# Linear attention and a squared-ReLU layer on one core: every SBUF tile begins 32 bytes past a multiple of 128

## The chip, the core and the metric

The kernel runs on one core of a Trainium2 chip. Five engines take part, each with its own list of instructions: TensorE (PE; its weight loads are listed apart as PEld), VectorE (DVE), ScalarE (ACT), GpSimd (POOL) and SyncE (SP), which here issues all transfers. SBUF is the on-chip memory of 128 partitions; a tile takes the same byte range in each partition, and that range's beginning is what this case is about. The metric is the device time of one execution in microseconds, median of three runs.

## The reference

Two stages follow each other. The first is linear attention over 4 batches, 4 heads, 1088 positions and 32 channels, with features that are products of two 8-wide projections (64 features). The second is a layer from 128 to 2048 and back, with `s * relu(h)**2 + b` between.

```python
def phi(x):
    a = np.einsum('rd,bhsd->bhsr', S1, x)
    b = np.einsum('rd,bhsd->bhsr', S2, x)
    return np.einsum('bhsi,bhsj->bhsij', a, b).reshape(*x.shape[:-1], r * r)
q_p, k_p = (phi(q), phi(k))
kv = np.einsum('bhsf,bhsd->bhfd', k_p, v)
z = np.sum(k_p, axis=2)
num = np.einsum('bhsf,bhfd->bhsd', q_p, kv)
den = np.einsum('bhsf,bhf->bhs', q_p, z)[..., None] + 1e-06
x = num / den            # then (4352 tokens, 128)
r = np.maximum(x @ w_in, 0.0)
out = (s * (r * r) + b) @ w_out
```

All inputs and the output are float32.

## The kernel before

The 4352 tokens are cut into nine tiles, one of 256 and eight of 512 columns; tokens lie along the free dimension. For each batch b, `kvphase` (L240 on) makes the features of k, multiplies them with v (L268, 33 columns of weights: 32 channels and a column of ones) and turns the result into the tile `st`. For each token tile t, `direct_features` or `stored_features` makes the features of q (the latter through a store `qd<-abq` and loads `pq<-qd`, `br<-qd`), `attend` multiplies them with `st` and divides, and leaves `x`, split as `xh` + `xl` in the type fp32r (L405). `ffn` then does eight steps of two 128-wide pieces of the hidden layer. From the second tile on, each piece takes three matmuls of 512 columns into `hp` (weights wil, wih, wih; streamed operands xh, xh, xl) and three into `ops` (weights wol, woh, woh; streamed uh, uh, ul), all on line 446. Between them ReLU (L127 or L129), square (L133 or L135), a cast to `uh` (L111) and the rest `ul = u - uh` (L440) run on ScalarE or VectorE, by the table `ON_DVE`. The first tile uses plain float32 weights, the tiles `w24`. The weights come in as 64-bit numbers (`raw`), are put together into w24 (L117 to L187) and split into wih, wil, woh and wol (L111, L425).

The order of all work is written out by hand in the table `ORDER`: each word advances one generator by a step, and each engine's list follows from it. The step `z` is a keep-warm matmul of 512 columns that reads a constant again and again (L512).

SBUF tiles are laid out in the order in which the pools `const`, `p1`, `p2`, `p3` and `p4` ask for them, one behind the other. The program's addresses (bytes within a partition) are, before the change:

| tiles, in order | start past a multiple of 128 | why |
|---|---|---|
| s_raw (640 bytes), cst_sb (640), sk (320) | 0 | the pool begins at a multiple of 128 |
| sq, srep, kvt, wih, wil, woh, wol, bias, w24, s_bits (320) | 64 | behind the 320 bytes of sk |
| st, ph, dt, rc, rr, kt, vt, pq, br, kab, x, abq, u, xh, xl, ot, qt, uh, ul, raw | 0 | behind the 320 bytes of s_bits |

From rr on, the last row's tiles begin at a multiple of 256, too (kt and vt, pq and br, u, xh, xl, ot, qt, uh, ul and raw among them). The tile vt is asked for with 1216 floats where 1188 are used, and bias with 32 where one is used, so that what follows keeps its start. Operands begin inside their tiles at multiples of 128 bytes, but for the pieces of vt: a piece of 33 floats follows the next at 132 bytes, and a batch's second group of chunks begins 2640 bytes in (1584 in the first batch).

Of the kernel before, what the change touches and what calls it, by code (L numbers as in the profile page):

```python
# [9 lines left out]
F32 = mybir.dt.float32  # L10
F32R = mybir.dt.float32r
BF16 = mybir.dt.bfloat16
I32 = mybir.dt.int32
# [6 lines left out]
P = 128  # L20
# [44 lines left out]
NS = 32 * 2 + 2 * R  # L65
# [24 lines left out]
def attn_ffn_kernel(ctx: ExitStack, tc: tile.TileContext, qT, kT, vp, s80, cst, w_in, w_out, outT):  # L90
    nc = tc.nc
    PSUM = bass.MemoryType.PSUM
    const = ctx.enter_context(tc.tile_pool(name="const", bufs=1))
# [100 lines left out]
    def to_float(key, out, raw, bits):  # L194
        low, high = words(raw)
        scaled(key + "m", out, f32(high), 2.0 ** -112)
        yield
        scaled_up(key + "b", bits, low.bitcast(U32), 0.875 * 2.0 ** -29, 0.4999)
        yield
        join(out.bitcast(I32), out.bitcast(I32), bits)  # L200
        yield
        with_sign(out.bitcast(I32), high, out.bitcast(I32))
        yield

    s_raw = const.tile([P, 2 * NS], I32, name="s_raw")
    cst_sb = const.tile([P, NCST], F32, name="cst_sb")
    s_col = cst_sb[:, CS:CS + 1]
    b_col = cst_sb[:, CB:CB + 1]  # L210
    spread = cst_sb[:, CT:CT + P]
    sk = const.tile([P, NS], F32, name="sk")
    sq = const.tile([P, 64], F32, name="sq")
    srep = const.tile([P, 2, 64], F32, name="srep")

    def s_phase():
        bits = const.tile([P, NS], I32, name="s_bits")
        yield from to_float("s", sk, s_raw, bits)
        own = sk[:, 64:].rearrange("p (w r) -> p w r", w=2)
        nc.vector.tensor_copy(out=srep[:, 1].rearrange("p (i x) -> p i x", i=R),  # L220
                              in_=own[:, 1].unsqueeze(1).broadcast_to([P, R, R]))
        yield
        nc.vector.tensor_copy(out=srep[:, 0].rearrange("p (i x) -> p i x", i=R),
                              in_=own[:, 0].unsqueeze(2).broadcast_to([P, R, R]))
        yield
        nc.gpsimd.tensor_copy(out=sq.rearrange("p (w i h) -> p w h i", w=2, i=R),
                              in_=sk[:, :64].rearrange("p (w h i) -> p w h i", w=2, h=H))
        yield
# [286 lines left out]
    with tc.manual_schedule():  # L515
        gens = {"z": keep_warm(), "Ls": load_s(), "s": s_phase(), "Lcst": load_constants()}
        for b in range(B):
            gens[f"Lk{b}"], gens[f"Lv{b}"], gens[f"k{b}"] = load_k(b), load_v(b), kvphase(b)
        for i in range(DFF // CW):
            for k in range(2):  # L520
                x = 2 * i + k
                gens[f"Lw{x}"], gens[f"w{x}"] = load_weights(i, k), split_weights(i, k)
        for t in range(NT):
            features = direct_features if t in DIRECT else stored_features
            gens[f"Lq{t}"], gens[f"q{t}"], gens[f"n{t}"] = load_q(t), features(t), attend(t)
            for jp in range(NPAIR):
                gens[f"{t}{jp}"] = ffn(t, jp)
        for c in ORDER.split():
            next(gens[c], None)
# [47 lines left out]
```

## Time and profile before

| | |
|---|---|
| median of three runs | 240.77 us (240.75 to 241.18) |
| the profiled execution | 240.83 us |
| its span, first to last instruction | 239.1 us |
| PE, DVE, ACT busy | 231.6, 201.0, 174.1 us |
| transfers | 22.15 MB, engines 30% busy over the span |

The span is what the profile shows; 1.73 us of the execution lie around it. A busy PE is counted by modelled ends, so the spacing of matmuls' starts says more than their durations. The page gives PE as nearly always busy, VectorE at 84%; the transfers crowd into the first 30 us, when the weights come in.

### The profile page before, as it was taken

Reading aid. Unit: us, or ns where it says so; the run is one execution under the profiler, and the core shown is the slowest. Engines: PE = TensorE matmul, PEld = TensorE weight load, DVE = VectorE, ACT = ScalarE, POOL = GpSimd, SP = SyncE. Lnnn points to the kernel's source line nnn. Section 1 sums busy time; section 2 is a strip of 40 time slices with the busy share of each in tenths; the row PEclk is TensorE's granted clock in tenths of the full one; section 3 lists DMA queues with packets and bytes.
Section 4 is the critical chain, followed back from the end, with each engine's and each line's share of the span. In section 5 each row is a group of like instructions: output and inputs, shape, how many; then the busy total and the mean of one; then the engine's idle time right before and its main releaser. Section 6 shows DMA issues by size and latency. Waiting matters only on the chain.

```text
span 239.1 us, 4347 instructions
## 1 busy us (share of the span) xinstructions
PE 231.6 (97%) x1750; PEld 177.9 (74%) x1750; DVE 201.0 (84%) x265; ACT 174.1 (73%) x203; POOL 4.2 (2%) x15
## 2 busy tenths in 40 slices
PE   7889999999999999999999999999999999999993
PEld 3647878787877778787778888787887788788882
DVE  2899999899699997789999997699468969989890
ACT  2289997897659959557586655897989793896771
POOL 1101100000000000000000000000000000000000
PEclk9999999999999999999999999999999999999999
DMA  6999823100492604810124001000430160001001
GB/s 173 314 410 406 273 58 116 57 0 3 133 197 76 162 16 145 195 47 3 44 85 118 0 3 57 31 4 22 134 86 3 54 180 7 4 0 44 0 3 44
DMA packets 9812, 22.15 MB, mean 93 GB/s; under 512 B 1088, under 2 KB 3520, under 8 KB 9792
## 3 DMA queue, kind: packets, MB, share of 16 engines
q1 hardware_dynamic: 9792, 21.87, 30.2%
q8 instruction: 14, 0.23, 0.4%
q14 instruction: 6, 0.05, 0.1%
HBM read 18.72 MB, written 3.15 MB: 91 GB/s over the span
## 4 chain that ended last, share of the span: by engine, by line
PE 94%; DVE 1%; DMA 1%; issue 1%; ACT 0%; SPq 0%; ACTq 0%
PE ops L446 41%; PE hp L446 41%; PE psa L368 4%; PE psa L268 3%; PE psa L247 2%; PE psa L327 2%; DMA kt<-kT 1%; PE hp L307 1%; DVE ph L254 1%; PE psa L283 1%; PE ops L512 0%; DVE kab L251 0%; ACT ot L500 0%; ACTq L573 0%; PE hp L368 0%
## 5 line engine op out<-in xcount | busy, mean ns | idle before, releaser
L440 DVE TENSOR_TENSOR ul<-u,uh 128x1024 fp32r<-128x1024 f32 x64 | 77.7, 1221 | 10.1 <-ACT uh L111 7.7
L129 ACT ACTIVATE u<-hp 128x1024 f32<-128x1024 f32 (+1 forms) x56 | 54.3, 969 | 26.4 <-PE hp L446 13.9
L135 ACT ACTIVATE u<-u 128x1024 f32<-128x1024 f32 (+1 forms) x61 | 61.1, 1004 | 10.7 <-DVE u L127 8.9
L446 PE MATMUL hp<-xh,wil 128*128 128x512 f32 x128 | 51.6, 403 | 0.0
L446 PE MATMUL ops<-uh,wol 128*128 128x512 f32 x128 | 51.3, 401 | 0.0
L446 PE MATMUL ops<-uh,woh 128*128 128x512 f32 x128 | 50.2, 392 | 0.0
L446 PE MATMUL hp<-xh,wih 128*128 128x512 f32 x128 | 50.2, 392 | 0.0
L446 PE MATMUL hp<-xl,wih 128*128 128x512 f32 x128 | 50.1, 392 | 0.0
L446 PE MATMUL ops<-ul,woh 128*128 128x512 f32 x128 | 39.8, 392 | 0.0
L111 ACT CAST uh<-u 128x1024 fp32r<-128x1024 f32 x33 | 34.7, 1051 | 3.8 <-DVE u L133 3.0
L446 PEld LDWEIGHTS ops<-uh,wol 128*128 128x128 f32 x128 | 24.0, 188 | 8.1 <-issue 1.8
L446 PEld LDWEIGHTS hp<-xh,wil 128*128 128x128 f32 x128 | 24.0, 188 | 7.4 <-issue 2.1
L446 PEld LDWEIGHTS hp<-xl,wih 128*128 128x128 f32 x128 | 24.0, 188 | 5.5 <-DVE xl L405 0.2
L446 PEld LDWEIGHTS ops<-ul,woh 128*128 128x128 f32 x128 | 23.9, 188 | 5.5 <-DVE ul L440 0.2
L446 PEld LDWEIGHTS ops<-uh,woh 128*128 128x128 f32 x128 | 24.1, 188 | 4.9
L446 PEld LDWEIGHTS hp<-xh,wih 128*128 128x128 f32 x128 | 24.1, 188 | 4.7
L111 DVE CAST uh<-u 128x1024 fp32r<-128x1024 f32 x31 | 21.3, 687 | 7.2 <-ACT u L135 6.4
L127 DVE TENSOR_SCALAR u<-hp 128x1024 f32<-128x1024 f32 (+1 forms) x16 | 19.0, 1189 | 1.8 <-PE hp L446 1.1
L133 DVE TENSOR_TENSOR u<-u 128x1024 f32<-128x1024 f32 x11 | 13.4, 1222 | 3.5 <-ACT u L129 3.3
L500 ACT ACTIVATE ot<-ops,bias,cst_sb 128x512 f32<-128x512 f32 (+1 forms) x10 | 7.1, 716 | 8.3 <-PE ops L446 8.2
L254 DVE TENSOR_TENSOR ph<-kab 128x768 f32<-128x768 f32 (+2 forms) x9 | 11.0, 1218 | 0.2
L368 PE MATMUL psa<-pq,st 64*32 64x256 f32 (+3 forms) x320 | 10.2, 345 | 0.6 <-issue 0.6
(63 smaller groups left out, 177.0 us busy)
## 6 DMA issues: line engine op xcount, KB each, us to landing
pq<-qd SPq DMA_DIRECT2D x7, 512.0 KB
br<-qd SPq DMA_DIRECT2D x14, 256.0 KB
qt<-qT SPq DMA_DIRECT2D x8, 256.0 KB
raw<-w_in SPq DMA_DIRECT2D x4, 512.0 KB
raw<-w_out SPq DMA_DIRECT2D x4, 512.0 KB
outT<-ot SPq DMA_DIRECT2D x7, 256.0 KB
vt<-vp SPq DMA_DIRECT2D x3, 330.0 KB
kt<-kT SPq DMA_DIRECT2D x3, 320.0 KB
```

Source lines behind the costliest of these rows:

```text
L111: (nc.vector.tensor_copy if key in ON_DVE else nc.scalar.copy)(out=out, in_=in_)
L127: nc.vector.tensor_scalar(out=out, in0=in_, scalar1=0.0, scalar2=None, op0=ALU.max)
L129: nc.scalar.activation(out=out, in_=in_, func=AF.Relu)
L133: nc.vector.tensor_tensor(out=out, in0=in_, in1=in_, op=ALU.mult)
L135: nc.scalar.activation(out=out, in_=in_, func=AF.Square)
L247: nc.tensor.matmul(ps[32 * q:32 * q + 32, w * w32:(w + 1) * w32], sk[:, 32 * w:32 * w + 32], kt[:, a:a + w32], start=(w == 0), stop=(w == ...
L254: nc.vector.tensor_tensor(out=ph[:, c0:c0 + n].rearrange("p c h i x -> p (c h) i x"), in0=a.unsqueeze(3).broadcast_to([P, H * n, R, R]), i ...
L268: nc.tensor.matmul(kvp[64 * g:64 * g + VW, 64 * j:64 * j + 64], v_in[b][:, c, h], ph[:, c, h].rearrange("p i x -> p (i x)"), start=(c == 0 ...
L368: nc.tensor.matmul(out[32 * h:32 * h + 32, e0:e1], st_t[b][64 * r:64 * r + 64, h // 2, h % 2, y], pq[64 * r:64 * r + 64, h, e0:e1], start= ...
L440: nc.vector.tensor_tensor(out=ul[:, :, :N], in0=u[:, :, :N], in1=f32(uh[:, :, :N]), op=ALU.subtract)
L446: nc.tensor.matmul(out, w, x, start=(first and k == 0), stop=(last and k == len(terms) - 1))
L500: nc.scalar.activation(out=ot[:, s], in_=o[:, s], func=AF.Identity, scale=s_col, bias=bias)
```

## The change

Three tiles ask for more room than they use: s_raw 32 bytes more (672 for 640), sk 384 bytes for 320, and s_bits 384 for 320. What is read and written in them stays. Everything behind s_raw moves by 32 bytes, behind sk by 96, behind s_bits by 160.

```diff
-    s_raw = const.tile([P, 2 * NS], I32, name="s_raw")
+    s_raw = const.tile([P, 2 * NS + 8], I32, name="s_raw")[:, :2 * NS]
...
-    sk = const.tile([P, NS], F32, name="sk")
+    sk = const.tile([P, 96], F32, name="sk")[:, :NS]
...
-        bits = const.tile([P, NS], I32, name="s_bits")
+        bits = const.tile([P, 96], I32, name="s_bits")[:, :NS]
```

Every tile behind s_raw then begins 32 bytes past a multiple of 128: those that were at 64 (weights, w24, sq, srep, kvt) and those that were at 0. Most of the tiles at a multiple of 256 now begin 160 past one. s_raw itself and the constants ahead of it, among them the one that the keep-warm matmuls read, stay where they are. The lists of instructions of all five engines are row for row the same as before, and so are the line numbers. PSUM is not touched.

## Rows read from the trace of the kernel before

**Rows 1.** The page: busy us (share) xinstructions, granted clock by slice, chain by engine.

```profile
span 239.1 us, 4347 instructions
...
PE 231.6 (97%) x1750; PEld 177.9 (74%) x1750; DVE 201.0 (84%) x265; ACT 174.1 (73%) x203; POOL 4.2 (2%) x15
...
PEclk9999999999999999999999999999999999999999
...
PE 94%; DVE 1%; DMA 1%; issue 1%; ACT 0%; SPq 0%; ACTq 0%
```

**Rows 2.** Stretches: us, busy us (xinstructions) by engine, granted clock, DMA share, GB/s.

```profile
4.00:8.00 4.00, 3.13 (x106) 2.28 (x105) 2.75 (x6) 0.65 (x2) 0.99 (x3) 1.00 0.95 299
8.00:12.00 4.00, 3.27 (x82) 2.38 (x81) 2.88 (x7) 1.01 (x3) 0.00 (x0) 1.00 0.94 316
12.00:16.00 4.00, 3.15 (x53) 1.40 (x44) 3.78 (x9) 3.61 (x8) 0.00 (x0) 1.00 1.02 406
16.00:20.00 4.00, 3.69 (x50) 2.15 (x49) 3.77 (x9) 3.13 (x7) 0.00 (x0) 1.00 1.03 419
20.00:30.00 10.00, 10.00 (x52) 8.80 (x47) 9.72 (x19) 9.84 (x18) 2.21 (x5) 1.00 0.94 319
30.00:60.00 30.00, 30.00 (x268) 23.11 (x268) 28.21 (x38) 25.11 (x33) 0.19 (x1) 1.00 0.16 47
60.00:90.00 30.00, 30.00 (x195) 22.61 (x194) 26.87 (x32) 21.59 (x23) 0.00 (x0) 1.00 0.46 116
...
180.00:210.00 30.00, 30.00 (x190) 22.71 (x189) 26.05 (x36) 23.21 (x25) 0.00 (x0) 1.00 0.18 49
```

**Rows 3.** Chain that ended last, in order of time: start us, us, what.

```profile
1.65 3.20 DMA kt<-kT
...
225.40 2.75 PE hp L446 x12
```

**Rows 4.** Timeline of PE: start us, us, engine, line, operation, tiles, shape, count.

```profile
15.31 0.82 PE L512 MATMUL ops<-const-bfloat16-1.0 128*128 128x512 bf16 x3
...
127.63 0.39 PE L446 MATMUL hp<-xh,wil 128*128 128x512 f32 x1
127.63 0.19 PEld L446 LDWEIGHTS hp<-xh,wih 128*128 128x128 f32 x1
...
127.86 0.39 PE L446 MATMUL hp<-xh,wih 128*128 128x512 f32 x1
...
130.38 0.39 PE L446 MATMUL ops<-uh,wol 128*128 128x512 f32 x1
```

**Rows 5.** Groups by line and shape: busy us, mean ns of one | idle before, releaser.

```profile
L440 DVE TENSOR_TENSOR ul<-u,uh 128x1024 fp32r<-128x1024 f32 x64 | 77.7, 1221 | 10.1 <-ACT uh L111 7.7
...
L446 PE MATMUL hp<-xh,wil 128*128 128x512 f32 x128 | 51.6, 403 | 0.0
...
L111 DVE CAST uh<-u 128x1024 fp32r<-128x1024 f32 x31 | 21.3, 687 | 7.2 <-ACT u L135 6.4 <-PE ops L446 0.4
...
L405 DVE TENSOR_TENSOR xl<-x,xh 128x512 fp32r<-128x512 f32 x8 | 5.5, 688 | 0.2
...
L425 DVE TENSOR_TENSOR wil<-w,wih 128x512 fp32r<-128x512 f32 x4 | 2.7, 686 | 0.0
...
L111 ACT CAST wih<-w 128x512 fp32r<-128x512 f32 x4 | 2.3, 611 | 0.0
L111 DVE CAST xh<-x 128x512 fp32r<-128x512 f32 x5 | 2.1, 425 | 0.1
...
L111 ACT CAST xh<-x 128x512 fp32r<-128x512 f32 x3 | 1.8, 609 | 0.3 <-DVE x L397 0.3
...
L111 DVE CAST woh<-w 128x512 fp32r<-128x512 f32 x1 | 0.4, 427 | 0.0
```

**Rows 6.** The tile vt: durations ns shortest/median/longest, first and last start us.

```profile
L268 PEld LDWEIGHTS psa<-ph,vt x288: 107/111/111, 7.3 to 142.0; 128*33 128x33 f32 x144
```

**Rows 7.** Stretches in which one kind of load runs (columns as in rows 2).

```profile
41.20:42.60 1.40, 1.40 (x7) 1.15 (x7) 1.40 (x2) 0.40 (x2) 0.00 (x0) 1.00 1.01 371
...
64.20:64.80 0.60, 0.60 (x5) 0.48 (x4) 0.53 (x1) 0.60 (x1) 0.00 (x0) 1.00 1.01 393
```

**Rows 8.** Timeline of transfers: first weights' issue and use, last stores' issue.

```profile
5.45 0.44 SPq L176 DMA_DIRECT2D raw<-w_in  x1
...
11.85 0.43 DVE L115 TENSOR_SCALAR w<-raw 128x512 f32<-128x512 f32 x1 [0.49 <-DMA raw<-w_in]
...
235.76 0.81 SPq L502 DMA_DIRECT2D outT<-ot  x2
```

## The prediction

> **What bounds the kernel now.** I read the page's busy shares and slices first. PE (TensorE) is busy 97% of a span of 239.1 us at the full granted clock in every slice, and the chain that ended last is PE for 94% [rows 1]. The table of stretches says where that holds: from 20 to 210 us PE is busy 10.00 of 10.00 and 30.00 of 30.00 us, stretch after stretch; only the first 20 us have gaps [rows 2]. From about 20 us on, therefore, a nanosecond added to each matmul is a nanosecond on the end, and a delay elsewhere costs only what the slack in front of PE doesn't absorb. That slack is thin on VectorE: 28.21 of 30 us busy from 30 to 60 us, 9.72 of 10 from 20 to 30 us [rows 2].
>
> The chain's last pieces show what PE does: twelve L446 matmuls take 2.75 us, 229 ns each [rows 3]. The single rows agree: from 127.63 to 130.38 us twelve such matmuls start, one every 0.23 us, each after its weight load of 0.19 us [rows 4]. There are 6 x 128 = 768 of them (the three groups of hp, and as many of ops) [rows 5]; 768 x 0.229 = 176 us, nearly three quarters of the span.
>
> **The change, part by part.** No instruction, wait, transfer or size is added or removed; each engine's list of work is the same. What changes is the start of nearly every operand within its partition. Weights, the tiles w24, sq, srep and kvt move from 64 to 32 past a multiple of 128 bytes; everything streamed past the weights, everything that VectorE and ScalarE stream, and every large transfer moves from 0 to 32 (160 past a multiple of 256 for most). So the sum has four terms, each of the form "does this unit care where an operand starts".
>
> (1) *VectorE and ScalarE.* The trace holds the same operation at two starts. The cast of 512 columns takes ScalarE 611 ns from w24 into wih (64 to 64) and 609 ns from x into xh (0 to 0); VectorE 427 ns and 425 ns; the subtraction 686 ns (wil, weights) and 688 ns (xl) [rows 5]. A shift of 64 bytes costs them 2 ns or less either way. No row has such a stream at 32. I take 0. The upper end: VectorE's cast of 1024 columns takes 687 ns where its subtraction takes 1221 [rows 5]; were the cast's double rate lost at these starts, 31 casts would gain 0.53 us each, 16.6 us on VectorE, most of which its idle 38 us take up. It stays as a rival.
>
> (2) *PE's weight loads.* The loads of v (L268) step by 33 floats, 132 bytes, so their 288 starts pass through every multiple of 4 bytes within 128, 32 among them. Shortest, median and longest are 107, 111 and 111 ns [rows 6]. The start of a weight load has no price here; and the large loads of 0.19 us lie beside a matmul of 0.23 us. I take 0.
>
> (3) *PE's streamed operand.* All 768 large matmuls stream from a start at 0 past 128; no row shows another start for them. This is the unknown that matters, since 1 ns on each is 768 x 1 = 0.77 us on the end. What bounds it: three keep-warm matmuls (L512), also 512 columns, at the same clock, take 0.82 us, of which the last shows 0.39: the two intervals before it are about 0.215 us [rows 4]. The large ones need 0.229, so something costs each about 14 ns beyond its columns. If that were a collision of the streamed read with the weight read, which now begin 64 bytes apart modulo 128 and afterwards at the same place, the new start could take all of it away (768 x 14 ns = -10.8 us). In the other direction, if reads come in pieces of 64 or 128 bytes, a 2048-byte row that begins 32 past a boundary touches one piece more. At 0.215 us for 512 columns, 16 columns (64 bytes) take 6.7 ns and 32 columns 13.4 ns: +5.2 or +10.3 us in all. I take 0 between these ends, by the nearest row: the weight loads, which read the same memory, show no trace of pieces at any start.
>
> (4) *Transfers.* The v loads are rows at awkward starts in the trace already: the second group of a batch of v lands 80 past a multiple of 128. While v loads alone run (41.2 to 42.6 us) the queues move 371 GB/s at a share of 1.01; while an aligned q load runs (64.2 to 64.8 us), 393 GB/s at 1.01 [rows 7]. That is 6% less, an upper end, because the source rows of v lie differently too. From 4 to 30 us the DMA engines are 94 to 103% busy [rows 2], so there it is of account. On the path lies the first kt load, 3.20 us [rows 3]: 6% is 0.2 us. Past that, the engines wait 0.5 us each for the first weights, issued from 5.45 us on and used at 11.85: 6% of 6.4 us is 0.4 us [rows 8]. Together at most 0.6 us, and less where PE's keep-warm matmuls and gaps of the first 16 us cover it (PE busy 3.13 to 3.27 of each 4 us [rows 2]). After 30 us the share falls to 16 to 46% [rows 2], and I take nothing there. Of the 0.6 I take 0.1, near the lower end, since the 32-byte step is kinder than the v rows' 16-byte one.
>
> The rows of the trace cannot price the far end of a store from SBUF, because every store of the kernel before begins at a multiple of 256. The Trainium skill, "DMA: Bandwidth & Descriptors", section "How a descriptor splits into AXI transactions", speaks against the change: a read that doesn't begin at a multiple of 256 bytes fetches from the boundary below, and the bytes before the start still cost beats. By its figures a 1024-byte row at 160 would need 37 beats for 32, an estimate of 16%; no run here shows it yet. As a mechanism of this kernel: the last stores are issued from 235.76 us for 0.81 us [rows 8], which leaves 2.5 us to the end of the span at 239.1; even a sixth of all of that would be 0.4 us, inside the forecast's own range below.
>
> Sum: 240.83 us (this execution: span 239.1 and 1.73 around it; the median of the runs is 240.77) + 0 + 0 + 0 + 0.1 = **240.9 us**, own range 240.4 to 241.3. A comparison of this kernel can tell about 0.2%, 0.48 us, from no change.
>
> **The rivals.**
> - *PE's reads come in pieces wider than 32 bytes* (the slower side). Place: each of the 768 large matmuls. Price: 6.7 ns (64-byte pieces) or 13.4 ns (128), so 246.0 or 251.1 us. It decides as soon as the 229 ns become 230: PE has no idle time to hide it. For it: a stream that already runs 14 ns over its columns is near some limit of its read path. Against: weight loads at every start take the same time [rows 6].
> - *Transfers suffer by the v loads' 6% or more.* Price: 0.6 us in the first 16 us as above, and up to 1.6 us (6% of the 26 us of full queues) if the late data reaches VectorE in its tight stretch from 20 to 30 us: 241.4 to 242.4.
> - *VectorE or ScalarE slows.* If the casts lose their double rate, the stretch from 30 to 60 us (3 such casts of uh and the 1.79 us that VectorE has free) is nearly full, later ones have more room; a local overrun of VectorE in a few tiles gives PE waits of some 2 us: 243.
> - *The change helps.* If the 14 ns are a collision that depends on where the weights begin against the streamed rows, equal starts could remove some or all: 230 to 240 us. For it: the starts of weights and streams do change against each other, by 64 bytes. Against: the interval is 229 ns for hp and ops alike, whichever buffer is read.
>
> **How the numbers follow.** No effect that can be measured: 0.52, the likeliest, for which the rows on VectorE, ScalarE and weight loads speak. Reads in pieces: 0.15 (0.10 at 64 bytes, 0.05 at 128). Transfers: 0.10. VectorE or ScalarE: 0.08. Faster: 0.15. Slower in all 0.33. The range leaves out the faster case (0.15) and the 128-byte piece (0.05): 240.2 to 246.2 us.
>
> **What would show it.** In the changed kernel's profile, twelve L446 matmuls at 2.75 us in the chain confirm term (3); 2.83 or 2.91 would be the pieces of 64 or 128 bytes, 2.6 the vanished collision. Casts at 611 and 425 ns and subtractions at 686 confirm (1); loads at 111 and 188 ns confirm (2). The kt load at 3.20 us and the first weights used at 11.85 us confirm (4). I am wrong if any of these moves with an unchanged list of instructions: then the start of an operand has a price, and the row that moved says whose.

## The result

The changed kernel takes 243.19 us (242.84 to 243.93) where the kernel before, on the same chip, takes 240.88 us: a ratio of 1.0098, 95% interval 1.0073 to 1.0124. Both are medians of four executions. It is slower, clear of the 0.2% that a comparison can tell. The time lies in the range of the prediction, but not in the case that it held the likeliest, "no effect".

The page of the changed kernel answers to [rows 1]: span, busy us, and the chain by engine.

```profile
span 241.4 us, 4347 instructions
...
PE 234.0 (97%) x1750; PEld 178.6 (74%) x1750; DVE 201.1 (83%) x265; ACT 174.2 (72%) x203; POOL 3.8 (2%) x15
...
PE 94%; DMA 2%; SPq 1%; issue 1%; ACT 0%; ACTq 0%
```

The reader is to see that only PE has grown: 231.6 to 234.0 us busy, while VectorE and ScalarE stand where they were (201.0 and 174.1 before). So nothing else became slower on the whole, and PE did so while working, not by waiting. Nor was it the clock: the granted clock is 1.00, the higher of its two levels (2.4 GHz), in the stretches of both kernels ([rows 2]; of the changed kernel, by the same columns, here).

```profile
30.00:60.00 30.00, 30.00 (x267) 22.98 (x266) 27.99 (x38) 24.91 (x33) 0.19 (x1) 1.00 0.15 47
...
180.00:210.00 30.00, 30.00 (x189) 22.53 (x188) 25.77 (x35) 23.73 (x25) 0.00 (x0) 1.00 0.18 49
```

Where in the span? The chain that ended last begins differently, with the load of qt (4.56 us) where the kernel before has the first load of kt (3.20 us, [rows 3]). The two chains come together by 17 us, 0.06 us apart, and the pieces below stand in both. Of the changed kernel (start, duration, what):

```profile
4.01 4.56 DMA qt<-qT
...
17.15 1.92 PE hp L446 x8
...
36.89 2.13 PE psa L268 x72
...
93.39 2.13 PE psa L268 x72
...
141.43 2.13 PE psa L268 x72
...
227.72 2.79 PE hp L446 x12
230.51 6.99 PE ops L446 x30
```

The same pieces of the kernel before (the one of 2.75 us is in [rows 3]):

```profile
17.09 1.92 PE hp L446 x8
...
36.80 2.13 PE psa L268 x72
...
92.66 2.13 PE psa L268 x72
...
140.15 2.13 PE psa L268 x72
...
228.15 7.00 PE ops L446 x30
```

The delay is 0.06 us at 17 us, then 0.09, 0.73, 1.28 and, at the last piece, 2.36 us. It is no single event; it grows with the large matmuls. The durations say the same: twelve large matmuls take 2.79 us instead of 2.75, while the attention's 72 small ones take 2.13 us in both and the first tile's eight float32 ones 1.92 us in both. From the starts of the single matmuls in the two traces, over the 722 neighbouring pairs of large ones that start less than 250 ns apart, the mean interval is 229.5 ns before and 232.5 after. Then 768 x 3.0 ns = 2.3 us, and the two profiled executions differ by 243.22 - 240.83 = 2.39 us. The whole loss is there. Only the last 30 matmuls, 7.00 against 6.99 us, don't differ: in the execution of before they were already as slow as the changed kernel's.

What stayed, as it answers to [rows 5]: the groups by line and shape of the changed kernel.

```profile
L440 DVE TENSOR_TENSOR ul<-u,uh 128x1024 fp32r<-128x1024 f32 x64 | 77.7, 1221 | 10.9 <-ACT uh L111 8.5
...
L111 DVE CAST uh<-u 128x1024 fp32r<-128x1024 f32 x31 | 21.3, 688 | 7.5 <-ACT u L135 6.6 <-PE ops L446 0.4
...
L405 DVE TENSOR_TENSOR xl<-x,xh 128x512 fp32r<-128x512 f32 x8 | 5.5, 690 | 0.2
...
L425 DVE TENSOR_TENSOR wil<-w,wih 128x512 fp32r<-128x512 f32 x4 | 2.7, 687 | 0.0
...
L111 ACT CAST wih<-w 128x512 fp32r<-128x512 f32 x4 | 2.3, 614 | 0.1
L111 DVE CAST xh<-x 128x512 fp32r<-128x512 f32 x5 | 2.1, 427 | 0.1
```

Every mean is within 3 ns of [rows 5]. The short weight loads of v, by the view of the tile vt, are those of [rows 6]:

```profile
L268 PEld LDWEIGHTS psa<-ph,vt x288: 107/111/111, 7.2 to 143.3; 128*33 128x33 f32 x144
```

And the first weights are used 0.06 us later than in [rows 8], by the timeline:

```profile
11.91 0.43 DVE L115 TENSOR_SCALAR w<-raw 128x512 f32<-128x512 f32 x1 [0.74 <-DMA raw<-w_in]
```

### The profile page after: what moved, and what is told of

Same layout as the page of the kernel before. It is cut to its first block, busy times and chain, and to the rows that moved or that the text cites. A ratio compares the mean times of both kernels' runs of the same rounds, so it can differ in the third digit from the quotient of the medians.

```text
span 241.4 us, 4347 instructions
## 1 busy us (share of the span) xinstructions
PE 234.0 (97%) x1750; PEld 178.6 (74%) x1750; DVE 201.1 (83%) x265; ACT 174.2 (72%) x203; POOL 3.8 (2%) x15
## 4 chain that ended last, share of the span: by engine, by line
PE 94%; DMA 2%; SPq 1%; issue 1%; ACT 0%; ACTq 0%
PE ops L446 41%; PE hp L446 41%; PE psa L368 4%; PE psa L268 3%; DMA qt<-qT 2%; PE psa L327 2%; PE psa L247 2%; PE hp L307 1%; PE psa L283 1%; SPq L153 1%; PE ops L512 0%; ACT ot L500 0%; ACTq L573 0%; PE hp L368 0%; SPq L162 0%
```

## The experiments

What is it about the large matmuls? In each, PE streams 512 columns past weights that are already in place, and loads the next matmul's weights meanwhile. Two operands have moved: weights from 64 to 32 past a multiple of 128 bytes, streams from 0 to 32. So three theories stood at the start. **A**: the streamed operand must begin at a multiple of 64 (the prediction's first rival). **B**: weights and stream must not begin at the same place modulo 128. **C**: the weights must begin at a multiple of 64. The pads of the three tiles place the two groups independently. All edits below are shown against the kernel before, added lines only where the rest is plain. Each run's reading is the duration of a chain piece of twelve large matmuls, 2.75 us before and 2.79 after, beside the time; its resolution of 0.01 us is 1 ns per matmul.

### Both groups, four placings

Weights at 32, streams at 0:

```diff
+    s_raw = const.tile([P, 2 * NS + 8], I32, name="s_raw")[:, :2 * NS]
+    sk = const.tile([P, 96], F32, name="sk")[:, :NS]
+        bits = const.tile([P, 88], I32, name="s_bits")[:, :NS]
```

> Weights and everything in the first pool at 32 past a multiple of 128, all streamed and loaded tiles at 0 as before. Theory A (the streamed operand of the 768 large matmuls has a price where it begins off a multiple of 64): interval 229 ns as before, 240.8 us. Rival B (weights and stream must not begin at the same place modulo 128): they begin 32 apart, so 229 ns and 240.8 us. Rival C (the start of the weights has the price): 232.5 ns as in the changed kernel, about 243.2 us.

Weights at 64 as before, streams at 32:

```diff
+        bits = const.tile([P, 88], I32, name="s_bits")[:, :NS]
```

> Weights at 64 as before, all streamed and loaded tiles at 32. Theory A: 232.5 ns per large matmul, 243.2 us. Rival B: starts are 32 apart, not equal: 229 ns, 240.8 us. Rival C: weights as before: 229 ns, 240.8 us.

Both at 0:

```diff
+    sk = const.tile([P, 96], F32, name="sk")[:, :NS]
+        bits = const.tile([P, 96], I32, name="s_bits")[:, :NS]
```

> Weights and streams both at 0 past a multiple of 128. Theory A: stream at a multiple of 64: 229 ns, 240.8 us. Rival B: equal starts as in the changed kernel: 232.5 ns, 243.2 us. Rival C: weights at a multiple of 64: 229 ns, 240.8 us.

Both at 64:

```diff
+        bits = const.tile([P, 96], I32, name="s_bits")[:, :NS]
```

> Weights and streams both at 64. Theory A with pieces of 64 bytes: 229 ns, 240.8 us; with pieces of 128 bytes a stream at 64 would cost as well: over 231 ns, over 242 us. Rival B: equal starts: 232.5 ns, 243.2 us. Rival C: 229 ns, 240.8 us.

Measured: 243.67 us (ratio 1.0118, 1.0102 to 1.0135), 243.77 (1.0120, 1.0100 to 1.0140), 243.00 (1.0087, 1.0069 to 1.0105) and 243.23 (1.0096, 1.0079 to 1.0113). All four are slower than before. One chain piece of each, in this order of runs; first weights at 32 and streams at 0:

```profile
228.17 2.80 PE hp L446 x12
```

Weights at 64, streams at 32, a piece on ops:

```profile
225.37 2.81 PE ops L446 x12
```

Both at 0, and after it both at 64:

```profile
227.65 2.79 PE hp L446 x12
```

```profile
227.68 2.79 PE hp L446 x12
```

All three theories fall. A and C fall with both at 0 or both at 64: everything begins at a multiple of 64, and it is slow. B fails in the first two runs, which begin 32 apart and are slower still. What the fast kernel alone has is a distance of 64 modulo 128 between weights and streams. That is theory **D**: the distance counts, and 64 is free of the price. Its rival **E**: the kernel before has the one good placing, weights at 64 and streams at 0.

### Sixty-four apart, elsewhere

The places exchanged, weights at 0 and streams at 64:

```diff
+    sk = const.tile([P, 96], F32, name="sk")[:, :NS]
```

> Weights at 0, streams at 64 past a multiple of 128: the places of the kernel before exchanged. Theory D (what counts is how far apart, modulo 128, the weights and the streamed operand of the large matmuls begin; 64 apart is free of the price): 229 ns, 240.8 us. Rival E (the kernel before has the one good placing: weights at 64 and streams at 0): 232 to 233.5 ns, about 243 us.

Weights at 32, streams at 96, which is the changed kernel with one of its three pads, that of s_bits, undone:

```diff
+    s_raw = const.tile([P, 2 * NS + 8], I32, name="s_raw")[:, :2 * NS]
+    sk = const.tile([P, 96], F32, name="sk")[:, :NS]
```

> Weights at 32, streams at 96: the changed kernel with one of its three pads (that of s_bits) undone. Nothing large begins at a multiple of 64. Theory D: 64 apart, 229 ns, 240.8 us. Rival E, and any theory in which 32 past a multiple of 64 is itself bad: 232 ns or more, 243 us or more.

Measured: 240.70 us (ratio 0.9998, 0.9982 to 1.0014) and 240.71 us (0.9989, 0.9970 to 1.0008). Both are as fast as the kernel before. The chain piece of the first, and of the second:

```profile
225.32 2.75 PE hp L446 x12
```

```profile
225.56 2.75 PE hp L446 x12
```

E falls, D stands. The second run decides more than that: each of its tiles behind s_raw begins 32 past a multiple of 64, all large transfers and all streams of VectorE and ScalarE included, and it costs nothing. So the start of a tile by itself has no price that this kernel can show.

One thing more lies in these layouts. The pads of the last two runs stand ahead of weights and streams alike and move both by the same amount, so weights and streams are as many bytes apart as in the kernel before, not only modulo 128. In the same way the three placings that are 0 apart have one distance in bytes among them, 64 more than before, and the two that are 32 apart another, 32 more. What these eight layouts show is therefore that the interval follows the distance in bytes, wherever the two groups lie. That distances which agree only modulo 128 are alike, they don't show.

### The weights alone

Only the four weight tiles of the large matmuls move, within their own tiles, by 32 bytes (and in the other run by 16, `4` in place of `8`); everything else keeps its place modulo 128:

```diff
-    wih = const.tile([P, DFF], F32R, name="wih")
+    wih = const.tile([P, DFF + 32], F32R, name="wih")[:, 8:8 + DFF]
...
```

> Only the four weight tiles of the large matmuls begin 32 bytes further within their own (wider) tiles, at 96; streams and all else at their place modulo 128. Theory D: 96 apart is as far from 64 as 32 is, so 233.3 ns as in the run with weights at 32 and streams at 0, 243.7 us, although nothing but these weights has moved. A theory on the streams or on transfers: 229 ns, 240.8 us.

> Only the four weight tiles begin 16 bytes further, at 80, streams at 0. Theory D with a price that grows with the distance from 64: between 229 and 233.3 ns, about 242 us. With steps of 32 bytes or more: 229 ns, 240.8 us.

Measured: 242.97 us (ratio 1.0093, 1.0066 to 1.0120) and 242.57 us (1.0075, 1.0051 to 1.0099). A chain piece of the run at 96, then of that at 80:

```profile
227.29 2.80 PE hp L446 x12
```

```profile
213.97 2.79 PE ops L446 x12
```

No stream, no transfer and no operand of another engine has changed its place modulo 128 in the run at 96, and the price is there: 232.6 ns, by the starts of the matmuls. Sixteen bytes are enough for most of it, 231.5 ns (the profile is of the shortest of that run's five executions, 241.94 us); so steps finer than 32 bytes count. Each widened tile also pushes what lies behind it by 128 bytes, so that modulo 256 not all four have moved alike: before, all four begin 192 past their streams; in the run at 96, wih and woh begin 224 past, wil and wol 96. By distance (weights less streams, modulo 128), all runs in one table; the interval is the mean over the starts of some 720 neighbouring large matmuls:

| weights, streams past 128 | apart | interval ns | median us |
|---|---|---|---|
| 64, 0 (before) | 64 | 229.5 | 240.88 |
| 0, 64 | 64 | 229.4 | 240.70 |
| 32, 96 | 64 | 229.4 | 240.71 |
| 80, 0 | 80 | 231.5 | 242.57 |
| 96, 0 | 96 | 232.6 | 242.97 |
| 64, 32 | 32 | 233.4 | 243.77 |
| 32, 0 | 32 | 233.4 | 243.67 |
| 0, 0 | 0 | 232.5 | 243.00 |
| 64, 64 | 0 | 232.5 | 243.23 |
| 32, 32 (the change) | 0 | 232.5 | 243.19 |

### Which matmul pays

If the distance counts because the next weights are read while a stream runs (**D1**), the interval ahead of the moved weights should grow; if a matmul pays for its own pair (**D2**), its own. Only wil is moved to 0, by 64 bytes within its tile:

```diff
-    wil = const.tile([P, DFF], F32R, name="wil")
+    wil = const.tile([P, DFF + 32], F32R, name="wil")[:, 16:16 + DFF]
```

> Only wil begins at 0 past a multiple of 128 (within its own tile), where the streams begin; wih, wol, woh stay at 64. A third of the hp matmuls have these weights. Theory D1 (the read of the next matmul's weights collides with the running stream): the interval of the matmul ahead of each wil matmul grows, above all that from hp<-xh... the last of a piece (xl with wih) to the next wil; intervals within ops stay at 229 ns; about 128 x 3 ns = 0.4 us or a little more, 241.2 us. Theory D2 (a matmul is slow where its own weights and its own stream begin at the same place): the interval that begins with the wil matmul grows instead; same sum.

And wil and wih together, so that hp has the bad distance and ops the good one:

> wil and wih begin at 0, where the streams begin; wol and woh stay at 64. Theory D: intervals within hp 232.4 ns, within ops 229 ns, half of the price of the run with weights and streams at 0: 384 x 3.1 ns = 1.2 us, 242.0 us. If the price came from anything that hp and ops share: both 231 ns or both as before.

Measured: 242.38 us (1.0064, 1.0043 to 1.0084) with wil alone, 241.23 us (1.0013, 0.9995 to 1.0030) with both. Chain pieces on ops and hp, first of the run with wil alone:

```profile
224.18 2.77 PE ops L446 x12
226.94 2.78 PE hp L446 x12
```

Then of the run with wil and wih:

```profile
222.89 2.75 PE ops L446 x12
225.64 2.77 PE hp L446 x12
```

The second run shows the price where its weights were moved and not elsewhere: hp grows to 2.77, ops stays at 2.75. But it is 0.02 us on twelve, half of what hp pays with all weights moved, and the time is hardly distinguishable from before. The first run missed on both counts. It costs 1.5 us, not 0.4. By the starts, the interval from wih back to wil within hp is 229.2 ns as before, and that from wil to wih 230.6; the one that grew is the next, from wih to wih, 234.4; and ops, whose weights had not moved, grew too, to 2.77 a piece. So neither D1 nor D2 holds as it was put, and D doesn't give the price of a layout in which the distances are mixed. Two things that the traces and addresses hold soften the case against D1. Of the intervals ahead of a wil matmul, the 29 that begin with ul and woh did grow, from 228.4 to 234.9 ns; the 86 from xl and wih didn't. And the widened wil pushes all that lies behind it, streams included, by 128 bytes: wih keeps its distance to the streams modulo 128, but goes from 192 to 64 modulo 256. That the interval from wih to wih grew may come from that; no run separates the two. For ops there is no such way out. The distance of wol and woh to their streams is in bytes that of before, and still ops grew, from 229.7 to 230.6 ns. A part of the price therefore carries over to matmuls whose own pair is as it was.

The single intervals fit that. For long stretches they repeat in a fixed order, 226, 229, 232 ns in the kernel before, whichever of the six kinds of matmul it is, and in longer orders such as 229, 237, 229, 238 or 230, 232, 241, 233 in the changed one.

### A weight load that does not walk

The last pair takes the walk of the weight read through memory away: one column loaded 128 times over (the products then lack the other 127 columns).

```diff
+    def col(w, c):
+        return w[:, c.start:c.start + 1].broadcast_to([P, P])
...
-                terms += [(wol[:, c], uh[:, i, :W]), (woh[:, c], uh[:, i, :W])]
+                terms += [(col(wol, c), uh[:, i, :W]), (col(woh, c), uh[:, i, :W])]
...
```

> The 768 large matmuls load one column of their weights 128 times over (step 0) instead of 128 columns, so that all products come out wrong and the weight load touches 4 bytes of a partition; loads, streams and order stay. Layout of the kernel before. If the excess over the columns (229 against about 215 ns) and the price of the layout both come from the weight read crossing the stream in memory: 215 to 218 ns, up to 768 x 12 ns = 9 us less unless VectorE then limits. If the excess belongs to every such matmul whatever it loads: 229 ns, 240.8 us.

> As the run with one column, in the layout of the changed kernel (all at 32 past a multiple of 128). If the price of the layout comes from the walk of the weight read through memory beside the stream: the same interval as the run with one column in the old layout. If it belongs to where the two begin, whatever is read after that: 3 ns more than that run.

Measured: 242.22 us in the old layout, 242.17 us in the changed one, spans of 240.2 us both. A chain piece of the one, and of the other:

```profile
226.60 2.77 PE hp L449 x12
```

```profile
226.52 2.78 PE hp L449 x12
```

The difference between the layouts is gone: 231.2 and 231.5 ns, between the good and the bad layout, and the two times are alike. Where both begin is not enough; the layout counted only where the load walks along the partition. But neither forecast of the first run came true, 215 to 218 ns or 229. The run is 0.6% slower than the kernel before (ratio 1.0057, 1.0036 to 1.0078), so loading one column over and over has a price of its own, which may hide some of the other. That walking weights cross the stream in memory is thus made likely, not shown. The excess over the columns stays: taking the walk away left 231 ns, not the 215 ns of [rows 4], and the hope of 9 us less was wrong.

## Why the prediction was right or wrong

*What bounds the kernel* was right. PE is saturated from 20 us on, and 3.0 ns on each of 768 matmuls came out at the end undiminished, 2.39 us.

*Term (1), VectorE and ScalarE, 0*: right. Their rows stayed within 3 ns, now with a row at 32 past 128.

*Term (2), weight loads, 0*: right as a duration, 111 and 188 ns as before, and misleading as a reason. That a load takes as long at every start says nothing on what it does to the stream beside it.

*Term (3), the streamed operand, 0*: this is the step that failed. It measured +3.0 ns per matmul, 2.3 us. "The nearest row" was the vt loads, 33 columns beside short float32 matmuls, and it priced how long a load takes, not what it does to the stream. The run with only the weights moved shows that what counts is a pair, and in the trace of before every large matmul had the same pair, 64 apart; so no row of that trace could give the price. One of the two bounds named the right quantity, where the weights begin against the stream, but with the sign reversed: it supposed that the kernel before was paying, and none of the layouts run is faster beyond the noise. The price was to be read as going either way. That a collision of the two reads lies behind it stays an inference.

*Term (4), transfers, 0.1*: right in size. The changed kernel's delay at 17 us is 0.06 us. The sign that was to confirm it, the kt load at 3.20 us on the path, can't be read, since the path now runs over qt. With every large transfer at 96 past 128, the time is that of before (0.9970 to 1.0008). That a 32-byte step is kinder to transfers than a 16-byte one, the reason for taking the lower end, no run shows. The last two stores show what a start off a multiple of 256 cost: their 256 packets of 1024 bytes take, by the trace, 45.8 ns each on average in the kernel before, 47.6 ns at 160 past a multiple of 256 in the changed one and 46.6 ns at 96 in the run with streams at 96. The prediction's estimate by *the rule of the Trainium skill* on such starts ("DMA: Bandwidth & Descriptors", "How a descriptor splits into AXI transactions") was 16% at 160. The trace has 4% there: for these reads from SBUF the rule is not borne out in its size.

*The rivals.* Reads in pieces (246.0 us): the right place, the wrong cause and twice the size; with both operands at multiples of 64 or 128 the price is there. Transfers and VectorE: no row moved by more than 0.06 us on the end. "The change helps": the right cause, the wrong sign. The four rivals had a chance of 0.48 between them, and slower 0.33; the range held because it was stretched to 246.2 us for reads in pieces, a cause that the runs refute. That the time lies in it is luck.

The Trainium skill, "SBUF — State Buffer", section "Who interferes with whom", gives PE two independent read ports, one for the stream and one for the weight load, and says that the port pair of VectorE and GpSimd is the only place of contention. The runs are hard to square with it: with only the weights moved against the streams, the interval rises from 229.5 to 232.6 ns, so stream and weight load are not without effect on each other. Where in the memory or in PE they meet, if they do, stays open, as does why the price carries over to matmuls whose own pair has not moved.

## What to carry to other kernels

Where PE is the bound and each matmul brings its own weights, the start of the weights against the start of the streamed operand is worth a look: here the distance of the kernel before (64 bytes modulo 128) is best of the five tried, and 32 bytes too much or too little cost about 1% of the whole. A pad between the two groups changes it, so a harmless resizing of a small tile can cost or gain that much; a pad ahead of both moves them together and cost nothing (240.70 and 240.71 us). Whether the same distance plus 128 is as good was not tried. Compare the interval of the large matmuls before crediting an edit. A row that shows one operand as indifferent does not price a pair.

## What the runs showed of the hardware that was not expected

- An interval of 229.4 to 229.5 ns between matmuls of 512 columns with weights and streams 64 bytes apart modulo 128; 232.5 ns at 0, 233.4 at 32, 232.6 at 96, 231.5 at 80. Layouts with one distance in bytes agree within 0.2 ns, wherever they lie.
- Starts 32 past a multiple of 64 cost this kernel nothing by themselves: 240.71 us with every tile behind s_raw placed so.
- The intervals are no noise. For long stretches they repeat in a fixed order (226, 229, 232 ns in the kernel before), and that order is not the order of the matmuls' kinds.
- The layout may be good and a stretch slow all the same: the last 30 matmuls of the kernel before take 7.00 us, 233 ns each. With the places exchanged they take 6.90, by the chain of that run:

```profile
228.07 6.90 PE ops L446 x30
```
